# Two buffers of a scan change places, an output copy gets four buffers instead of two, and three small pieces of work move between engines

## The chip, the cores and the metric

The kernel runs on one core of a Trainium2 chip. The core has a matrix engine (PE, with its weight loads shown as PEld), a vector engine (DVE), a scalar engine (ACT), a general engine (POOL), and SyncE (SP), whose queue issues most of the DMA transfers here. Each engine works through its own instructions in order and waits for others by semaphores. The metric is device time in microseconds (us). A part of the time lies around the profiled span, from the first to the last instruction.

## What is computed

Two independent parts, whose results stand side by side in the output (1 x 2048 x 896, bf16). S = 2048 positions, D = 448 features.

Part A is a state-space convolution with complex diagonal state:

```
Lam_bar = exp(dt * Lam);  B_bar = ((Lam_bar - 1) / Lam) * B
Bu = x @ B_bar^T
for t in range(2048):
    h = Lam_bar * h + Bu[t];  hs.append(h)
y = 2 * real(hs @ C^T) + x * Dskip
```

Part B is attention in which a position sees eight positions at distances 0, 2, ..., 14 behind it, with 16 heads of 28 features:

```
q, k, v = split(x @ wqkv)
logits[s, w] = q[s] . k[s - 2 w] / sqrt(28)     (s - 2 w >= 0)
out = (sum over w of softmax(logits)[s, w] * v[s - 2 w]) @ wo
```

## The kernel before, in words

Both parts share one core and are woven together by hand. Part B's projections for q and k run first (`proj_t`), then v (`proj`), with DVE making the products q x k (`products`, L312) and PE summing them over the features of a head (`sums`, L323). `softmax` works on one half `hf` of the positions at a time: PE turns the logits (tile `lgs`, L355), DVE takes the maximum, ACT the exponential into tile `e` (L364), PE sums, and DVE multiplies `e` with the reciprocal into `attn` (L374). `pv` is DVE's main work: for each quarter of the positions, eight multiplications of `attn` with `vd` (L414) and seven additions (L417). A finished quarter is turned by a DMA transpose into `oT` (`tail`, L430), multiplied with `wo` on PE (`wo_ps`, L437), copied by ACT into a buffer `yb` (two buffers; the last quarter writes into places of `ya` instead) and stored from SP's queue (L441). One quarter makes four such copies and stores (`i` and `odd`).

Part A holds 448 complex states in seven groups `m`, and reads the positions as 512 columns of four consecutive positions `b`. Level 1 (`level1_halves`, `level1`) builds for `b` = 0 to 3 the state inside a group of four from PE matmuls (L130, L638, L642), copied into `h` by ACT. `scan` carries states over the columns: for the groups 0 to 3, then 4 and 5, then 6, it sums four columns on PE (L673, L676), ACT copies them into the first of a pair of tiles `pbuf` (L678), and in seven steps PE adds the tile shifted by 1, 2, 4, ... columns (L683), and ACT copies the result to the other tile of the pair (L686). Tiles with one tag share one place in memory; the next tile of that place may be written when the last reader of the tile before is done. The first scan's pair lives in the places of `e` and `lgs`; the other scans' pairs have their own. POOL clears a strip in front of each `pbuf` (L628). `ends` makes the remaining columns (`gt`, L702) into `G`; `setup_c` makes the output matrix `Ccat` (L613).

`correct(b, m, eng)` then adds to `h[b]` of group `m` what comes from earlier columns: a matmul with `G` (L711). With `eng` "V", DVE adds the result to `h` (L715). With "A", PE adds `h` itself by a second matmul with the identity (L710), and ACT copies the sum back (L713). `y` makes the output of a quarter of the columns: the skip term with the diagonal `Dg` (L727), seven matmuls with `Ccat` (L731), ACT's copy into `ya` (L734), a store (L735). `Dg` is made in `skip`: PE turns the row Dskip (L583), one engine copies it to `dsk` (L585), ACT scales the identity with it (L588).

Order of the work: PE's instructions are chained by hand (`chain`; `lanes` for the projections; the list `line` at the end). In the last stage `line` holds seven corrections by ACT, the second quarter's `wo` matmuls, the `y` sums for `b` = 3, 0, 1, the third quarter's, `y` for 2 and the last quarter's; one correction for DVE is put in after each 1.55 us of estimated PE work. DVE's instructions of the last two quarters are chained too (`vchain`); `each` counts them, and from the fifth on sets a correction behind each. What is not chained is ordered by a planner when the kernel is built, from priorities (the order in the program) and its own estimates of time; it writes each engine's queue, SP's too, so a different program can give a different order.

Of the kernel before, what the change touches and what calls it, by code (L numbers as in the profile page):

```python
# [15 lines left out]
bf16 = mybir.dt.bfloat16  # L16

S = 2048
D = 448
T = 16  # L20
NCH = 128
# [13 lines left out]
NM = 7  # L35
# [3 lines left out]
PAD = 64  # L39
# [121 lines left out]
class PartB:  # L161
# [260 lines left out]
    def tail(self, hf, jl0, acc, last):  # L422
        nc, pool, cx = self.nc, self.pool, self.cx
        if self.oT is None:
            self.oT = pool.tile([KA, 2, 14, NCH], bf16, name="oT", tag="bX")
        oT, flat = self.oT[:, self.oi % 2], acc.rearrange("p j d h -> p (j d h)")
        self.oi += 1
        n = 7 if last else 14
        for c in range(0, 14, n):
            nc.sync.dma_start_transpose(oT[:, c:c + n], flat[:, c * KA:(c + n) * KA])  # L430

        def out(i):
            done = []
            for odd in range(2):
                ps = cx.ps([NCH, D], f32, "wo_ps", "lg")
                for k in range(KT):
                    done.append(nc.tensor.matmul(ps[:], lhsT=oT[:, 7 * i + 3 * odd + k, :], rhs=self.wo_p[:, odd, k, :],  # L437
                                                 start=(k == 0), stop=(k == KT - 1)).ins)
                yb = cx.ya[:, 4 + 2 * i + odd] if last else pool.tile([NCH, D], bf16, name="yb", tag="yb", bufs=2)[:]
                cx.ev("V" if last and odd else "A", yb, ps[:])  # L440
                nc.sync.dma_start(self.out_b[:, hf * HJ + jl0 + 2 * i + odd, :], yb)  # L441
            return done

        return out if last else lambda: [out(i) for i in range(2)]


class PartA:
# [132 lines left out]
    def skip(self):  # L580
        nc, ident = self.nc, self.cx.ident
        ptd = self.cx.ps([KA, KT], bf16, "pt_d", "lg")
        self.cx.chain(nc.tensor.transpose(ptd[:], self.drow[:], ident[0:KT, 0:KT]).ins)  # L583
        dsk = self.pool.tile([KA, KT], f32, name="dsk")
        nc.vector.tensor_copy(dsk[:], ptd[:])  # L585
        self.Dg = self.pool.tile([KA, KT, KA], bf16, name="Dg")
        for k in range(KT):
            nc.scalar.activation(self.Dg[:, k, :], ident[:], ACT.Copy, scale=dsk[:, k:k + 1])  # L588
# [32 lines left out]

    def alloc_scan(self):
        pool = self.pool
        self.pbuf = [[pool.tile([NCH, m1 - m0, PAD + NCH], bf16, name=f"pbuf{m0}{i}", tag=f"pbuf{m0}{i}" if m0 else ("e", "lgs")[i]) for i in range(2)]
                     for m0, m1 in MH]
        for pb in self.pbuf:
            for t_ in pb:
                self.cx.order(self.nc.gpsimd.memset(t_[:, :, 0:PAD], 0.0).ins, self.cx.relay, "NoSync")  # L628
        self.G = pool.tile([NCH, NM, 2 + NF], bf16, name="G", tag="q0")
        self.cx.order(self.nc.gpsimd.memset(self.G[:, :, 0:1], 0.0).ins, self.cx.relay, "NoSync")  # L630
# [109 lines left out]
def body(ctx: ExitStack, tc: tile.TileContext, A_x, A_Lre, A_Lim, A_Bre, A_Bim, A_Cre, A_Cim, A_logdt, A_Dskip,  # L740
         B_x, B_wqkv, B_wo, out):
    nc = tc.nc
    pool = ctx.enter_context(tc.tile_pool(name="sb", bufs=1))
    psum = ctx.enter_context(tc.tile_pool(name="ps", bufs=1, space=bass.MemoryType.PSUM))
    out_v = out[0].rearrange("(p j) e -> p j e", j=T)
    cx = Ctx(tc, pool, psum)
    b = PartB(cx, B_x, B_wqkv, B_wo, out_v[:, :, D:2 * D])
    a = PartA(cx, A_x, A_Lre, A_Lim, A_Bre, A_Bim, A_Cre, A_Cim, A_logdt, A_Dskip, out[0].rearrange("(n b) e -> n b e", b=4)[:, :, 0:D])
# [98 lines left out]
        a.ends(mh)  # L847
    cx.ya = pool.tile([NCH, 8, D], bf16, name="ya", tag="cn")
    line, extra, steps = [], [], []
    todo = [(b_, m) for b_ in (1, 2) for m in range(NM)]  # L850

    def each(ins):
        cx.vchain(ins)
        steps.append(ins)
        if len(steps) >= 5 and todo:
            extra.extend(a.correct(*todo.pop(0), "V"))

    def wo_line(lists):
        return [(i, 0.19) for l_ in lists for i in l_]

    for m in range(NM):
        line += a.correct(0, m, "A")
    line += wo_line(wo[1]())
    deque(b.pv(0, at0, 0, 4, each=each), 0)
    deque(b.pv(0, at0, 4, 8, True, each=each), 0)
    for b_, r in itertools.product((3, 0, 1, 2), range(4)):
        line += a.y(r, b_)
# [41 lines left out]
```

## Time and profile before

| | |
|---|---|
| median of 3 runs | 150.92 us (150.15 to 151.6) |
| the profiled execution | 150.87 us |
| its span | 148.9 us |
| PE busy | 137.5 us, 1258 matmuls |
| DVE busy | 124.5 us, 156 instructions |
| ACT busy | 90.1 us, 197 instructions |
| POOL busy | 10.5 us |
| mean granted PE clock | 0.989 |

A line of the order of time gives start, duration, engine, line of the kernel, operation, output and inputs with their size, and in brackets the idle time of the engine before it with what ended it. Consecutive instructions of one form are merged ("x6"). A line of the table of waits gives the engine and line that waited, the one it waited for, the total in us, how often, and the longest. A line for a stretch A:B gives its length, then busy time and count for PE, PEld, DVE, ACT and POOL, then the granted PE clock (1.00 is full), the DMA engines' share and GB/s.

### The profile page before, as it was taken

What the parts mean: (1) busy time and instruction counts of PE and PEld (TensorE: products, weight loads), DVE (VectorE), ACT (ScalarE), POOL (GpSimd) and SP (SyncE); (2) the same over time, 40 slices, a digit from 0 to 9 for tenths busy, and PEclk for the clock granted to TensorE, in tenths of its full rate; (3) what the DMA queues carried; (4) which work ended last, traced back from release to release, by engine and by line L of the source; (5) the groups of instructions that cost most, each with busy time, mean ns of one, the idle gap of its engine ahead of it and who ended that gap; (6) DMA issues with size and microseconds to landing.
All of it is one profiled execution on the core that took longest, in us unless ns stands there. A gap on an engine that the chain in (4) does not pass through costs nothing.

```text
span 148.9 us, 3301 instructions
## 1 busy us (share of the span) xinstructions
PE 137.5 (92%) x1258; PEld 78.3 (53%) x1258; DVE 124.5 (84%) x156; ACT 90.1 (61%) x197; POOL 10.5 (7%) x108
## 2 busy tenths in 40 slices
PE   6999999999999989999789999929999999999971
PEld 2565435445666555466455556518656555555430
DVE  4689639989999889999999999940799999999411
ACT  3668685878585685635599978646963233354320
POOL 7211000000000001000020000000000000000000
PEclk9999999999999999999999999996999999999999
DMA  4999899899948699900033000341013128123473
GB/s 111 316 206 132 207 188 143 160 129 207 189 97 168 109 241 253 218 1 0 0 64 64 0 0 0 74 122 57 0 43 112 63 57 194 62 92 122 67 203 106
DMA packets 45166, 17.03 MB, mean 114 GB/s; under 512 B 37267, under 2 KB 44769, under 8 KB 45151
## 3 DMA queue, kind: packets, MB, share of 16 engines
q1 hardware_dynamic: 44586, 16.36, 53.3%
q10 hardware_dynamic: 565, 0.46, 1.2%
q8 instruction: 10, 0.16, 0.5%
q14 instruction: 5, 0.04, 0.1%
HBM read 3.91 MB, written 3.67 MB: 51 GB/s over the span
## 4 chain that ended last, share of the span: by engine, by line
PE 67%; DVE 18%; ACT 6%; DMA 4%; issue 2%; POOL 0%; ACTq 0%; DVEq 0%; POOLq 0%
PE qk_ps L130 16%; PE y_ps L731 14%; PE wo_ps L437 5%; DVE pvb L414 5%; PE l L638 5%; PE v_ps L130 5%; PE lg L323 4%; DVE pvb L417 4%; PE gt L702 3%; PE co L711 3%; PE warm L73 2%; DVE pr L312 2%; ACT pbuf L686 2%; PE y_ps L727 2%; DMA out_dram<-yb 2%; DMA oT<-pvb 2%
## 5 line engine op out<-in xcount | busy, mean ns | idle before, releaser
L414 DVE TENSOR_TENSOR pvb<-attn,vd 128x1792 bf16<-128x1792 bf16 (+1 forms) x33 | 34.3, 1062 | 0.0
L417 DVE TENSOR_TENSOR pvb<-pvb 128x1792 bf16<-128x1792 bf16 (+1 forms) x29 | 30.7, 1060 | 0.3
L130 PE MATMUL qk_ps<-xbT,wqkv_nat 64*128 64x512 bf16 (+1 forms) x210 | 24.0, 335 | 0.7 <-POOL spot L139 0.3
L312 DVE TENSOR_TENSOR pr<-q,kd 128x3072 bf16<-128x3072 bf16 x11 | 19.1, 1756 | 3.5 <-ACT q L156 3.1
L731 PE MATMUL y_ps<-Ccat,h 128*128 128x448 bf16 x84 | 18.5, 353 | 0.0
L734 ACT CAST ya<-y_ps 128x448 bf16<-128x448 f32 x16 | 8.5, 532 | 16.4 <-PE y_ps L731 15.8
L130 PEld LDWEIGHTS <-wqkv_nat 64*128 64x128 bf16 x210 | 11.1, 94 | 10.5 <-POOL spot L139 3.1
L130 PE MATMUL l1h<-xaT,Bcat 64*128 64x512 bf16 x112 | 15.4, 377 | 0.0
L715 DVE TENSOR_TENSOR h<-co,h 128x512 bf16<-128x512 f32 x14 | 9.7, 690 | 6.5 <-PE co L711 6.5
L437 PE MATMUL wo_ps<-wo_p,oT 128*128 128x448 bf16 x64 | 14.0, 352 | 1.1 <-ACT ya L734 0.6
L638 PE MATMUL l<-xaT,Bcat 128*128 128x512 bf16 x48 | 13.6, 379 | 0.0
L130 PE MATMUL v_ps<-wqkv_nat,xbT 64*128 64x448 bf16 x112 | 13.1, 361 | 0.0
L156 ACT CAST kd<-qk_ps 128x512 bf16<-128x512 f32 (+4 forms) x26 | 10.4, 423 | 4.5 <-PE qk_ps L130 4.3
L156 ACT CAST q<-qk_ps 128x512 bf16<-128x512 f32 (+2 forms) x23 | 9.9, 455 | 1.7 <-PE qk_ps L130 1.4
L156 ACT CAST yb<-wo_ps 128x448 bf16<-128x448 f32 x12 | 6.5, 542 | 6.6 <-DMA out_dram<-yb 4.5
L683 PE MATMUL l<-pbuf,mat 128*128 128x127 bf16 (+6 forms) x49 | 6.4, 223 | 4.4 <-ACT pbuf L686 3.0
L686 ACT CAST pbuf<-l 128x512 bf16<-128x512 f32 (+2 forms) x21 | 8.8, 420 | 2.5 <-PE l L683 2.4
L731 PEld LDWEIGHTS <-h 128*128 128x128 bf16 x84 | 7.4, 98 | 5.4
L156 ACT CAST vd<-v_ps 128x448 bf16<-128x448 f32 x16 | 7.6, 528 | 3.7 <-PE v_ps L130 3.5
L312 DVE TENSOR_TENSOR kd<-q,kd 128x3072 bf16<-128x3072 bf16 x5 | 8.8, 1756 | 1.2 <-ACT q L156 1.2
L130 PEld LDWEIGHTS <-Bcat 64*128 64x128 bf16 x112 | 7.0, 94 | 5.3 <-issue 0.4
L139 POOL MEMSET spot<- 1x1 f32 x63 | 5.6, 88 | 58.9 <-PE qk_ps L130 25.4
(133 smaller groups left out, 216.6 us busy)
## 6 DMA issues: line engine op xcount, KB each, us to landing
out_dram<-ya SPq DMA_DIRECT2D x20, 112.0 KB, 1.7
out_dram<-yb SPq DMA_DIRECT2D x12, 112.0 KB, 1.7
vd<-vd SPq DMA_DIRECT2D x1, 784.0 KB, 5.8
wqkv_nat<-in_B_wqkv_dram SPq DMA_DIRECT2D x2, 336.0 KB
vd<-vd SPq DMA_DIRECT2D x1, 588.0 KB
xn<-in_B_x_dram SPq DMA_DIRECT2D x2, 224.0 KB, 3.4
cn<-in_A_C_re_dram SPq DMA_DIRECT2D x4, 98.0 KB, 3.0
cn<-in_A_C_im_dram SPq DMA_DIRECT2D x4, 98.0 KB, 3.4
```

Of the source, the lines that this page charges most:

```text
L130: ins = mm(g["ps"], lhsT=l_, rhs=r_, start=first, stop=not (g["left"][0] or g["left"][1]), skip_group_check=True).ins
L156: return self.nc.scalar.copy(out, in_).ins
L312: self.queued(V.tensor_tensor(pr, q[0][:, qu].unsqueeze(2).to_broadcast([KA, KT - 1, 4, n]), self.shifted(self.kT[:, 2 * i + qu], s), op=A ...
L414: each(V.tensor_tensor(t_[:, c0:c1], at[:, w, jl0 + c0:jl0 + c1, :].unsqueeze(2).to_broadcast([NCH, c1 - c0, DH, H]), self.vd[:, off + c0: ...
L417: ins = V.tensor_tensor(acc[:, c0:c1], acc[:, c0:c1], t_[:, c0:c1], op=ALU.add).ins
L437: done.append(nc.tensor.matmul(ps[:], lhsT=oT[:, 7 * i + 3 * odd + k, :], rhs=self.wo_p[:, odd, k, :], start=(k == 0), stop=(k == KT - 1)) ...
L638: nc.tensor.matmul(ps[:], lhsT=self.Bcat[:, m, k, :], rhs=self.xT[:, b, k, :], start=(k == 0), stop=(b == 0 and k == KT - 1))
L683: nc.tensor.matmul(ps[:, m - m0, shf:], lhsT=M[T << s_][:, m, :], rhs=src[:, m - m0, PAD:PAD + NCH - shf], start=False, stop=True, skip_gr ...
L686: nc.scalar.copy(dst[:, :, PAD:], ps[:])
L715: cx.vchain(nc.vector.tensor_tensor(h, ps[:], h, op=ALU.add).ins)
L731: out.append(nc.tensor.matmul(ps[:], lhsT=self.state(m, r, b), rhs=self.C[:, m, :], start=False, stop=(m == NM - 1), skip_group_check=True ...
L734: nc.scalar.copy(ya, ps[:])
```

## The change

Five edits. The output copies of part B get four buffers `yb` instead of two. The copy of the skip row goes from DVE to ACT. The first scan's pair changes places: its first tile now lies where `lgs` was and its second where `e` was. The two corrections (1, 0) and (1, 1) leave DVE's list, 14 long before and 12 now, and are made by ACT behind its seven. DVE's first correction comes behind the seventh counted step of part B instead of the fifth.

```diff
-                yb = cx.ya[:, 4 + 2 * i + odd] if last else pool.tile([NCH, D], bf16, name="yb", tag="yb", bufs=2)[:]
+                yb = cx.ya[:, 4 + 2 * i + odd] if last else pool.tile([NCH, D], bf16, name="yb", tag="yb", bufs=4)[:]
...
-        nc.vector.tensor_copy(dsk[:], ptd[:])
+        nc.scalar.copy(dsk[:], ptd[:])
...
-        self.pbuf = [[pool.tile([NCH, m1 - m0, PAD + NCH], bf16, name=f"pbuf{m0}{i}", tag=f"pbuf{m0}{i}" if m0 else ("e", "lgs")[i]) for i in range(2)]
+        self.pbuf = [[pool.tile([NCH, m1 - m0, PAD + NCH], bf16, name=f"pbuf{m0}{i}", tag=f"pbuf{m0}{i}" if m0 else ("lgs", "e")[i]) for i in range(2)]
...
-    todo = [(b_, m) for b_ in (1, 2) for m in range(NM)]
+    todo = [(b_, m) for b_ in (1, 2) for m in range(NM)][2:]
...
-        if len(steps) >= 5 and todo:
+        if len(steps) >= 7 and todo:
...
-    for m in range(NM):
-        line += a.correct(0, m, "A")
+    for b_, m in [(0, m) for m in range(NM)] + [(1, 0), (1, 1)]:
+        line += a.correct(b_, m, "A")
```

## The prediction

> **What bounds the kernel now.** I read the page's first and fourth parts, then the table of waits, then the instructions in order of time around the largest waits.
>
> ```profile
> span 148.9 us, 3301 instructions
> ...
> PE 137.5 (92%) x1258; PEld 78.3 (53%) x1258; DVE 124.5 (84%) x156; ACT 90.1 (61%) x197; POOL 10.5 (7%) x108
> ...
> PE 67%; DVE 18%; ACT 6%; DMA 4%; issue 2%; POOL 0%; ACTq 0%; DVEq 0%; POOLq 0%
> ```
>
> PE is busy 137.5 of 148.9 us and makes two thirds of the chain that ended last. So the time is the PE's work plus the places at which PE stands still or runs slowly, unless DVE (124.5 us) comes to end later than PE. The table of waits (total, times, longest) names those places:
>
> ```profile
> DVE h L715 <- PE co L711: 6.5, 1, 6.5
> ...
> ACT yb L156 <- DMA out_dram<-yb: 4.5, 4, 2.9
> ...
> ACT pbuf L678 <- DVE attn L374: 1.8, 1, 1.8
> ```
>
> Behind both of ACT's waits stands one of PE. In order of time, the later pair, which is the larger:
>
> ```profile
> 94.29 1.53 SPq L430 DMA_TRANSPOSE oT<-pvb  x1
> ...
> 95.87 15.17 SPq L441 DMA_DIRECT2D out_dram<-yb  x6
> ...
> 97.43 1.09 DVE L417 TENSOR_TENSOR pvb<-pvb 128x1792 bf16<-128x1792 bf16 x1
> 98.99 0.53 ACT L156 CAST yb<-wo_ps 128x448 bf16<-128x448 f32 x1 [2.90 <-DMA out_dram<-yb]
> ...
> 99.74 0.21 PE L683 MATMUL l<-pbuf,mat 128*128 128x112 bf16 x1 [2.87 <-ACT pbuf L686]
> ```
>
> The third `yb` copy finds both buffers taken. The first buffer's store stood in SP's queue behind the transpose, began at 95.87 and released ACT at 98.99. The in-order ACT held the last scan's `pbuf` copies behind that copy, and PE waited 2.87 us for them. DVE finished its fifth step of part B at 97.43 + 1.09 = 98.52 and then waited 6.50 us for the first correction.
>
> **The change part by part.** Everything is taken off or put on 150.87 us, the profiled execution's own time (span 148.9, so 1.97 lie around it); the median of the three runs shown is 150.92.
>
> *Four `yb` buffers.* The four copies of a pass (two `i`, two `odd`) no longer reuse a buffer, so the wait on a store goes from this pass; the next pass comes over 10 us later (behind the correction casts, which end at 109.01 by a row below), when those stores have landed. Both copies that waited remain, at 0.53 us each on ACT, in front of scan copies. PE gains at most its 2.87 us, and at least 2.87 - 2 x 0.53 = 1.81 if the two casts now delay the scan in full. I take **-2.87**: in the stretch below ACT (the fourth pair of columns) was busy 1.49 of 4 us, so the casts find room there.
>
> ```profile
> 94.00:98.00 4.00, 2.72 (x19) 1.59 (x17) 3.93 (x5) 1.49 (x5) 0.00 (x0) 1.00 0.70 144
> ```
>
> *The clock behind that wait.* One form of `gt` matmul, before and after the clock recovers:
>
> ```profile
> 100.68 0.52 PE L702 MATMUL gt<-h,ident 128*128 128x384 bf16 x1
> ...
> 104.03 0.33 PE L702 MATMUL gt<-h,ident 128*128 128x384 bf16 x1
> ```
>
> It takes 0.52 us at first and 0.33 later. The stretches below give the granted clock in the column behind POOL: 0.61 right behind the wait, 0.98 after.
>
> ```profile
> 92.77:109.01 16.24, 13.21 (x89) 8.94 (x88) 9.67 (x12) 11.40 (x30) 0.00 (x0) 0.89 0.24 58
> ...
> 98.98:103.05 4.07, 3.31 (x23) 2.62 (x23) 0.00 (x0) 3.08 (x10) 0.00 (x0) 0.61 0.19 59
> 103.05:108.39 5.34, 5.34 (x36) 3.59 (x35) 3.36 (x5) 4.98 (x11) 0.00 (x0) 0.98 0.00 1
> ```
>
> PE was busy 3.31 us there, and would have needed 3.31 x 0.61 / 0.98 = 2.06 at the later clock: 1.25 us. ACT, though, was busy 3.08 of those 4.07 us with the copies that these matmuls feed, so some of it will not show. Between 0 and -1.25 I take **-0.7**.
>
> The Trainium skill, "TensorE: Matmul & The Clock Gate", in "What's actually happening", lets the clock fall only after an idle window of about 3.4 us. By that rule an idle of 2.87 us would cost no clock, this term would be 0 and the sum 146.1. The rows above differ from it: the clock was 0.61 behind a wait of 2.87 us.
>
> *The scan's homes.* `pbuf` 0 of the first scan lay in the home of `e`, which the multiplication into `attn` reads last; it moves to the home of `lgs`, whose last readers are the `lt` matmuls near 55 us (quoted with the skip row below).
>
> ```profile
> 71.99 0.53 ACT L156 CAST Ccat<-c_ps 128x448 bf16<-128x448 f32 x1
> ...
> 73.53 0.69 DVE L374 TENSOR_TENSOR attn<-e,rec 128x1024 bf16<-128x1024 bf16 x1
> ...
> 74.31 0.58 ACT L678 CAST pbuf<-l 128x512 bf16<-128x512 f32 x1 [1.78 <-DVE attn L374]
> ...
> 74.94 0.28 PE L683 MATMUL l<-pbuf,mat 128*128 128x127 bf16 x2 [1.38 <-ACT pbuf L678]
> ...
> 75.63 0.62 ACT L686 CAST pbuf<-l 128x512 bf16<-128x512 f32 x1
> ```
>
> The first copy (74.31) can start 1.78 us earlier; now the second copy (75.63) is the one that needs `e`, and it can start at 74.31, 1.32 us earlier. The clearing of the padding on POOL takes the same two homes in the same order, and no scan step reads it. PE loses its wait of 1.38 but may wait some tenths at the second step. Behind it both are full (3.92 and 3.94 of 4 us):
>
> ```profile
> 78.00:82.00 4.00, 3.92 (x29) 2.29 (x28) 4.00 (x6) 3.94 (x9) 0.00 (x0) 1.00 0.37 69
> ```
>
> So what they gain at the start is carried along, unless DVE, which doesn't get earlier, delivers the late steps' `mat` tiles just in time. Bounds 0 and -1.78; I take **-1.2**.
>
> *Two more corrections on ACT.* Each takes two matmuls instead of one:
>
> ```profile
> 104.55 0.38 PE L711 MATMUL co<-G,mat 128*128 128x512 bf16 x1
> ...
> 104.98 0.38 PE L711 MATMUL co<-G,mat 128*128 128x512 bf16 x1
> 105.03 0.69 DVE L715 TENSOR_TENSOR h<-co,h 128x512 bf16<-128x512 f32 x1 [6.50 <-PE co L711]
> 105.40 3.61 ACT L713 CAST h<-co 128x512 bf16<-128x512 f32 x7
> ```
>
> From 104.55 to 104.98 PE makes two of them, so a correction with one matmul more costs 0.215 us more, two of them **+0.43** on PE. On ACT two casts of 3.61 / 7 = 0.52, 1.03 in all. In 92.77 to 109.01 ACT was busy 11.40 of 16.24 us; with 12.43 in a stretch shortened by the terms above to about 13.1 it is nearly full. Behind these casts wait `yb` copies of the next pass and the buffers of the first `y` sums; that is a rival below.
>
> *Corrections later.* DVE does two steps of about 1.06 us inside the 6.50 us in which it stood. It reaches its first correction at 98.52 + 2.1 = 100.6, and PE's first `co` would come at 104.55 - 2.87 - 0.7 - 1.2 = 99.8, so DVE waits no more. Its later work shrinks by those two steps and by two corrections of 0.6 (start to start of its pieces below):
>
> ```profile
> 109.90 0.69 DVE L715 TENSOR_TENSOR h<-co,h 128x512 bf16<-128x512 f32 x1
> 110.50 1.09 DVE L417 TENSOR_TENSOR pvb<-pvb 128x1792 bf16<-128x1792 bf16 x1
> ```
>
> It ends at 139.61 - 4.4 - 2.1 - 1.2 = 131.9 instead of 139.61. That is no term by itself, since PE ends later; it pays at the end:
>
> ```profile
> 138.99 0.62 DVE L417 TENSOR_TENSOR pvb<-pvb 128x896 bf16<-128x896 bf16 x1
> ...
> 141.12 1.23 SPq L430 DMA_TRANSPOSE oT<-pvb  x1
> ...
> 141.83 1.25 PEld L437 LDWEIGHTS <-oT 128*128 128x128 bf16 x8 [1.04 <-DMA oT<-pvb]
> 141.83 1.69 PE L437 MATMUL wo_ps<-wo_p,oT 128*128 128x448 bf16 x8 [0.60 <-ACT ya L734]
> ...
> 144.03 1.69 PE L437 MATMUL wo_ps<-wo_p,oT 128*128 128x448 bf16 x8 [0.52 <-DMA oT<-pvb]
> ```
>
> PE's last two groups wait 0.60 and 0.52 us, each for a transpose (the second one landed 2.9 us after its issue). The first wait is put down to a `ya` copy that ended at the same moment; the weight load beside it names the transpose. With DVE done 7 us earlier and PE 4 to 5, the transposes land first: **-1.12** (bounds 0, if SP's queue keeps them behind late stores, and -1.12).
>
> *The skip row's copy on ACT.*
>
> ```profile
> 54.37 0.15 DVE L585 CAST dsk<-pt_d 128x4 f32<-128x4 bf16 x1
> ...
> 54.57 0.41 PE L355 MATMUL lt<-ident,lgs 128*128 128x128 bf16 x4 [0.46 <-DVE dsk L585]
> ...
> 54.62 1.28 ACT L588 ACTIVATE Dg<-ident,dsk 128x128 bf16<-128x128 bf16 x4 [0.23 <-DVE dsk L585]
> ```
>
> ACT sat idle 0.23 us before `Dg`, waiting for this very copy, so it can make it within a few tenths of the same moment. If it runs earlier, PE gains up to its 0.46; if a `vd` copy of 0.5 stands in front, PE loses as much. I take 0, with -0.46 and +0.5 as ends.
>
> Sum: -2.87 - 0.7 - 1.2 + 0.43 - 1.12 = -5.46, so 150.87 - 5.46 = **145.4 us**. All best ends give -2.87 - 1.25 - 1.78 + 0.43 - 1.12 - 0.46 = -7.05, or 143.8; all worst ends -1.81 + 0.43 + 0.5 = -0.88, or 150.0.
>
> **The rivals.**
>
> *Only the buffer wait goes.* ACT, nearly full, becomes what paces PE between 92 and 105 us, and the start won at the scan is lost again before it. Then the clock and homes terms are 0 and half of the tail's stays: -2.87 + 0.43 - 0.56 = -3.0, so 147.9. For it speaks ACT at 12.43 of 13.1 us; against it that PE's four `co` buffers let it run ahead of ACT by some 2 us.
>
> *It doesn't do what it says.* The third copy is free of its buffer but the order that the planner writes leaves other waits of the same size, say behind PE's `wo_ps` sums: about 150.4. Against it: ACT's release at 98.99 stands 3.1 us after the store's issue, and the last of those sums was made well before:
>
> ```profile
> 95.63 0.54 PE L437 MATMUL wo_ps<-wo_p,oT 128*128 128x448 bf16 x2
> ```
>
> *Slower: the first scan starves PE.* The planner writes the order of each engine anew. With the first copy free from 72.5 us it can set the scan's steps ahead of the level-1 matmuls which now fill the pauses between steps:
>
> ```profile
> 76.43 0.41 PE L683 MATMUL l<-pbuf,mat 128*128 128x126 bf16 x4
> ...
> 77.79 0.41 PE L683 MATMUL l<-pbuf,mat 128*128 128x124 bf16 x4
> ```
>
> A step comes 1.36 us after the one before and uses 0.41 of PE; 0.95 is filled. Empty in all seven steps, that is 6.65 us on PE, and the homes term goes: 145.4 + 1.2 + 6.65 = 153.3. It decides in favour of slower from (153.3 - 150.87 = 2.4 less) 4.2 us of such gaps, or 0.6 a step. Against it: code and priorities of the two kinds of work are unchanged, and the PE now interleaves them evenly.
>
> **How the numbers follow.** A forecast within 143.8 to 147.2 gets 0.64, only the buffer wait (147.2 to 149.4) 0.20, no effect 0.07, slower 0.08; 0.01 is below. The range takes the first two: 143.8 to 149.2. About 1%, 149.4 and 152.4, is what a measurement can tell from no change. Faster 0.85, same 0.07, slower 0.08.
>
> **What would show it.** Right: no `yb` copy waits for a store near 95 us; no PE wait over 1 us between 92 and 105, and a granted clock near 1 there; the first `pbuf` copy starts near 72.6 and the second near 74.3; first `co` near 99.8; DVE's wait ahead of its first correction under 1 us; DVE's last step near 132; no wait of the last two `wo_ps` groups for a transpose. Wrong: PE gaps between the first scan's steps, ACT without idle time from 92 on with PE waiting for it, or the last transposes issued behind late `ya` stores.

## The result, and the profile after

The changed kernel took 145.52 us in the median of four runs (145.12 to 145.92), against 150.53 for the kernel before: a ratio of 0.966, with a 95% interval of 0.960 to 0.972. The forecast was 145.4 in a range of 143.8 to 149.2. The profiled execution took 145.12 us. In the table of the experiments the medians are of all executions, while the ratios leave out four that ran slow: two of the changed kernel with two buffers, one of the kernel before with its homes exchanged (473.77 us) and one of the kernel before.

The page after, and its waits (total, times, longest):

```profile
span 143.2 us, 3302 instructions
...
PE 137.2 (96%) x1260; PEld 78.0 (54%) x1260; DVE 123.2 (86%) x153; ACT 90.9 (63%) x200; POOL 10.5 (7%) x108
```

```profile
ACT yb L156 <- PE wo_ps L437: 2.3, 8, 0.4
...
PEld L683 <- DVE mat L607: 0.7, 1, 0.7
```

PE does the same work, and two matmuls more, in 5.7 us less span: its share rose from 92 to 96%. No `yb` copy waits for a store any more, no wait on `attn` stands in front of the first scan copy, and the only new wait of a scan step is one on a `mat` tile. In order of time, the first scan, the `yb` copies, the first corrections and the end:

```profile
73.39 0.59 ACT L678 CAST pbuf<-l 128x512 bf16<-128x512 f32 x1 [0.26 <-PE l L676]
...
74.20 0.69 DVE L374 TENSOR_TENSOR attn<-e,rec 128x1024 bf16<-128x1024 bf16 x1
...
74.98 0.59 ACT L686 CAST pbuf<-l 128x512 bf16<-128x512 f32 x1
...
94.48 0.53 ACT L156 CAST yb<-wo_ps 128x448 bf16<-128x448 f32 x1
...
96.54 3.36 SPq L441 DMA_DIRECT2D out_dram<-yb  x4
...
99.74 0.39 PE L711 MATMUL co<-G,mat 128*128 128x512 bf16 x1
...
100.24 1.09 DVE L417 TENSOR_TENSOR pvb<-pvb 128x1792 bf16<-128x1792 bf16 x1
...
101.24 0.68 DVE L715 TENSOR_TENSOR h<-co,h 128x512 bf16<-128x512 f32 x1
...
131.43 2.57 SPq L430 DMA_TRANSPOSE oT<-pvb  x2
131.94 0.62 DVE L417 TENSOR_TENSOR pvb<-pvb 128x896 bf16<-128x896 bf16 x1
...
135.34 1.49 PE L731 MATMUL y_ps<-Ccat,h 128*128 128x448 bf16 x7
...
136.67 3.31 PE L437 MATMUL wo_ps<-wo_p,oT 128*128 128x448 bf16 x16
```

The third `yb` copy starts at 94.48, two microseconds before any store of this pass is issued (96.54). DVE reaches its first correction without idle time. Both last transposes are issued together, and PE runs the last sixteen `wo_ps` matmuls as one piece, with no wait.

This execution reached `attn` at 74.20, the one before at 73.53; the first 70 us differ by such tenths from one execution to the next. So distances from `attn` are compared below. To the first correction: before 104.55 - 73.53 = 31.02 us, after 99.74 - 74.20 = 25.54, a gain of 5.48. Two stretches from the first `yb` copy to the first correction, the first of before, the second of after (length; busy time of PE, PEld, DVE, ACT, POOL; PE's clock):

```profile
92.77:104.55 11.78, 8.74 (x68) 6.45 (x66) 5.68 (x6) 7.05 (x22) 0.00 (x0) 0.86 0.34 80
```

```profile
92.36:99.74 7.38, 7.16 (x67) 5.49 (x66) 7.31 (x8) 6.77 (x22) 0.00 (x0) 1.00 0.48 110
```

Of the 11.78 - 7.38 = 4.40 us, PE's idle time gives 3.04 - 0.22 = 2.82, and its busy time, for the same matmuls (68 and 67 records of them), 8.74 - 7.16 = 1.58: the clock was 0.86 in one stretch and 1.00 in the other.

### The profile page after: what moved, and what is told of

Its sections match the earlier page's. It is cut to its first block, busy times and chain, and to the rows that moved or that the text cites. A ratio compares the mean times of both kernels' runs of the same rounds, so it can differ in the third digit from the quotient of the medians.

```text
span 143.2 us, 3302 instructions
## 1 busy us (share of the span) xinstructions
PE 137.2 (96%) x1260; PEld 78.0 (54%) x1260; DVE 123.2 (86%) x153; ACT 90.9 (63%) x200; POOL 10.5 (7%) x108
## 4 chain that ended last, share of the span: by engine, by line
PE 69%; DVE 23%; ACT 3%; issue 2%; POOL 0%; DVEq 0%; ACTq 0%; POOLq 0%
PE qk_ps L130 16%; PE y_ps L731 15%; DVE pvb L414 8%; PE wo_ps L437 7%; DVE pvb L417 6%; PE v_ps L130 5%; PE lg L323 5%; PE l L638 5%; PE co L711 3%; PE warm L73 3%; DVE pr L312 2%; DVE mat L607 2%; PE y_ps L727 2%; PE gt L702 2%; PE l L683 2%
## 5 line engine op out<-in xcount | busy, mean ns | idle before, releaser
L731 PE MATMUL y_ps<-Ccat,h 128*128 128x448 bf16 x84 | 17.9, 353 | 0.0
L130 PEld LDWEIGHTS <-xbT 64*128 64x128 bf16 x112 | 7.3, 145 | 4.1 <-issue 1.3
L437 PEld LDWEIGHTS <-oT 128*128 128x128 bf16 x64 | 6.0, 98 | 5.5 <-issue 0.6
L649 ACT CAST h<-l1h 128x512 bf16<-128x512 f32 x12 | 6.3, 602 | 3.5 <-PE l1h L130 3.5
```

The costliest lines, as they stand in the source:

```text
L130: ins = mm(g["ps"], lhsT=l_, rhs=r_, start=first, stop=not (g["left"][0] or g["left"][1]), skip_group_check=True).ins
L649: self.nc.scalar.copy(h, ps)
L731: out.append(nc.tensor.matmul(ps[:], lhsT=self.state(m, r, b), rhs=self.C[:, m, :], start=False, stop=(m == NM - 1), skip_group_check=True ...
```

## The experiments

Twelve kernels ran, in three groups, each group beside the kernel before on its own chip. "Two" and "four" are the `yb` buffers; "homes" are the exchanged homes; "corrections" are nine by ACT, twelve by DVE, from the seventh step. The kernel before has one median in each group. That of the last is lower because fewer of its executions there had the drop of the clock (see "The clock by itself"), so between groups the times compare better than the ratios.

| kernel | median us | before, same chip | ratio, 95% interval |
|---|---|---|---|
| the changed kernel again | 145.38 | 151.27 | 0.963 (0.959 to 0.966) |
| changed, homes as before | 146.39 | 151.27 | 0.970 (0.966 to 0.974) |
| changed, seven and fourteen corrections | 145.78 | 151.27 | 0.965 (0.961 to 0.969) |
| changed, all corrections as before | 146.52 | 151.27 | 0.970 (0.966 to 0.974) |
| changed, two buffers | 151.55 | 151.36 | 1.002 (0.998 to 1.005) |
| before, homes exchanged | 151.31 | 151.36 | 1.003 (0.999 to 1.007) |
| before, four buffers | 147.31 | 151.36 | 0.974 (0.970 to 0.978) |
| before, PE kept busy in the wait | 149.72 | 151.36 | 0.990 (0.987 to 0.993) |
| before, first stores from ACT's queue | 146.95 | 150.38 | 0.974 (0.969 to 0.979) |
| before, corrections of the change | 151.25 | 150.38 | 1.005 (1.001 to 1.008) |
| changed, skip row's copy on DVE | 144.93 | 150.38 | 0.961 (0.957 to 0.964) |
| changed, eight and thirteen corrections | 144.85 | 150.38 | 0.960 (0.957 to 0.964) |

### The buffers: alone, and taken away

Alone on the kernel before:

```diff
-... name="yb", tag="yb", bufs=2)[:]
+... name="yb", tag="yb", bufs=4)[:]
```

> The kernel before with four yb buffers and nothing else. Theory: the buffer wait of 2.9 us and most of the slow clock behind it (1.25) go, 4.1 to 4.4 us on PE up to the first correction; but DVE is then the later one at the end, as it still waits for its first correction and has all fourteen: it ends about 4 us earlier than before, so the last transposes stay as late against PE as they were and the tail's waits of 1.1 us stay. 146.2 to 146.5. Rival (the clock drop is covered by ACT's copies): 147.4 to 147.7.

Measured: 4.0 us faster (147.31 against 151.36). The time lies between the theory's 146.2 to 146.5 and the rival's 147.4 to 147.7. From the order of time and a stretch of this kernel:

```profile
74.14 0.68 DVE L374 TENSOR_TENSOR attn<-e,rec 128x1024 bf16<-128x1024 bf16 x1
...
100.76 0.39 PE L711 MATMUL co<-G,mat 128*128 128x512 bf16 x1
...
138.31 1.69 PE L437 MATMUL wo_ps<-wo_p,oT 128*128 128x448 bf16 x8 [0.86 <-DMA oT<-pvb]
...
140.70 1.69 PE L437 MATMUL wo_ps<-wo_p,oT 128*128 128x448 bf16 x8 [0.71 <-DMA oT<-pvb]
```

```profile
93.38:100.76 7.38, 7.16 (x68) 5.49 (x66) 5.68 (x6) 6.76 (x22) 0.00 (x0) 1.00 0.53 126
```

The first correction comes 100.76 - 74.14 = 26.62 us behind `attn`: 4.40 earlier than before, at the upper end of what was expected, with the clock at 1.00. The waits at the end not only stay, they are 1.57 us instead of 1.12, which takes 0.45 of it back. That, and a kernel before that took 151.36 here instead of the 150.87 from which the theory counted, is what its time missed; the rival's reason, a clock drop covered by ACT's copies, is not borne out.

The changed kernel with two buffers, the same line the other way round:

> The changed kernel with two yb buffers again. Theory (the third yb copy is tied through the first store to the transpose in front of it in SP's queue, and that to DVE, which the change does not make earlier): the wait of ACT comes back and is longer than 2.9 us by the 1.1 us that PE and ACT now arrive earlier, the granted clock falls again, the first correction comes near 104.5 whatever the scan gained; of the change only the tail's 1.4 us less 0.43 for ACT's corrections remains: 149.5 us. Rival (the terms add up independently): the scan's 1.1 us stays too, 148.4.

Measured: 151.55, no faster than before, and 2 us above the theory. In order of time:

```profile
98.95 0.53 ACT L156 CAST yb<-wo_ps 128x448 bf16<-128x448 f32 x1 [3.60 <-DMA out_dram<-yb]
...
135.25 2.57 SPq L430 DMA_TRANSPOSE oT<-pvb  x2
...
137.91 1.02 SPq L441 DMA_DIRECT2D out_dram<-yb  x2
...
141.98 0.53 ACT L156 CAST yb<-wo_ps 128x448 bf16<-128x448 f32 x1 [4.36 <-DMA out_dram<-yb]
```

The first wait is back as expected, longer (3.60 us instead of 2.90). What was not expected is a second one: with DVE done earlier, the planner puts both last transposes ahead of three of the third quarter's four stores in SP's queue, and with two buffers ACT stands 4.36 us on such a store, with three `ya` copies behind it. So four buffers are worth 4.0 us alone and about 6 us (151.55 - 145.38) in the changed kernel.

The corrections alone on the kernel before show the same thing from the other side:

```diff
-    todo = [(b_, m) for b_ in (1, 2) for m in range(NM)]
+    todo = [(b_, m) for b_ in (1, 2) for m in range(NM)][2:]
...
-        if len(steps) >= 5 and todo:
+        if len(steps) >= 7 and todo:
...
-    for m in range(NM):
-        line += a.correct(0, m, "A")
+    for b_, m in [(0, m) for m in range(NM)] + [(1, 0), (1, 1)]:
+        line += a.correct(b_, m, "A")
```

> The kernel before with the corrections of the change alone (nine by ACT, twelve by DVE from its seventh step), two buffers, old homes. Theory (DVE's earlier end lets the planner set the last transposes ahead of yb stores in SP's queue; with two buffers ACT then stands on a store again, near the end): ACT waits 3 to 5 us for a store behind the last transposes and the time is that of before or longer, 150.5 to 152. Rival (the tail's waits of 1.1 us go at the price of 0.43): 149.9 to 150.6, no wait on a store over 1.5 us near the end.

Measured: 151.25 us, 1.005 of before. That is no loss: the clock drop was in nine of these ten executions, but in only seven of the 17 of the kernel before on this chip, and those seven have a median of 151.28. The wait near the end is there:

```profile
135.53 2.57 SPq L430 DMA_TRANSPOSE oT<-pvb  x2
...
138.19 1.02 SPq L441 DMA_DIRECT2D out_dram<-yb  x2
...
141.70 0.53 ACT L156 CAST yb<-wo_ps 128x448 bf16<-128x448 f32 x1 [3.82 <-DMA out_dram<-yb]
```

### Is it the number of buffers or the place in the queue?

The kernel before with two buffers; only the first pass's four stores change their queue:

```diff
-                nc.sync.dma_start(self.out_b[:, hf * HJ + jl0 + 2 * i + odd, :], yb)
+                (nc.scalar if (hf, jl0) == (1, 0) else nc.sync).dma_start(self.out_b[:, hf * HJ + jl0 + 2 * i + odd, :], yb)
```

> The kernel before with two yb buffers, but the first pass's four stores are issued from ACT's queue instead of SP's, so that they don't stand behind the transpose. Theory (the wait came from the place of the store in SP's queue, not from two buffers being too few): each store starts right behind its copy, lands within 3 us, ACT waits at most 1 us for a buffer, the clock stays up, first correction near 101 to 102, time 147 to 148.5, like four buffers alone (147.3) or up to 1 us behind, for four issues of about 0.4 us on ACT. Rival (a store takes too long for two buffers wherever it is issued): the wait stays at 2 to 3 us, 149.5 to 151.5.

Measured: 146.95 us, where four buffers gave 147.31 on another chip. The first store is issued behind its copy, ahead of the transpose:

```profile
93.65 0.53 ACT L156 CAST yb<-wo_ps 128x448 bf16<-128x448 f32 x1
94.26 0.36 ACTq L441 DMA_DIRECT2D out_dram<-yb  x1
95.16 1.53 SPq L430 DMA_TRANSPOSE oT<-pvb  x1
...
96.92 0.65 ACT L156 CAST yb<-wo_ps 128x448 bf16<-128x448 f32 x1
```

In the kernel before, the same copy and DVE's last addition of that quarter stood so:

```profile
92.77 0.53 ACT L156 CAST yb<-wo_ps 128x448 bf16<-128x448 f32 x1
...
93.16 1.10 DVE L417 TENSOR_TENSOR pvb<-pvb 128x1792 bf16<-128x1792 bf16 x1
```

The copy was done at 93.30, the addition at 94.26; the transpose went out at 94.29 and the store behind it at 95.87, 2.57 us behind the copy. In this pass two buffers were enough for stores that leave at once. The cause of the wait was a store that had to pass a transpose which itself waited for DVE; four buffers cover that, and another queue removes it. The order of PE's work changed in this kernel too (one correction came ahead of the last `gt` groups), so its first correction is not compared with the others'.

### The clock by itself

The kernel before, with PE kept busy in the wait by thirteen matmuls on zeros, whose sums nobody reads; the wait itself stays.

```diff
...
+        for i in range(13):
+            ins = nc.tensor.matmul(wp[:], lhsT=cx.wz[:, 0:NCH], rhs=cx.wz[:], start=True, stop=True).ins
+            cx.order(ins, prev, "NoSync")
+            prev = ins
...
```

> The kernel before, with thirteen more matmuls on zeros (2.8 us, their sums are not used) in PE's queue where it waits for the yb buffer. The wait of ACT stays. Theory (the slow clock behind the wait costs about 1 us by itself): the granted clock stays near 1 behind the wait, the gt groups take 0.5 us each instead of 1.0, the first correction comes 0.7 to 1.3 us earlier and the time is 0.7 to 1.3 us shorter, 149.3 to 149.9. Rival (ACT's copies pace that stretch, the clock is covered): within 0.3 us of before.

Measured: ratio 0.990, 1.5 us faster than before. In order of time, and a stretch:

```profile
73.89 0.68 DVE L374 TENSOR_TENSOR attn<-e,rec 128x1024 bf16<-128x1024 bf16 x1
...
97.07 2.97 PE L889 MATMUL warm<-wz 128*128 128x512 bf16 x12
99.33 0.53 ACT L156 CAST yb<-wo_ps 128x448 bf16<-128x448 f32 x1 [2.87 <-DMA out_dram<-yb]
...
100.13 0.32 PE L702 MATMUL gt<-h,ident 128*128 128x384 bf16 x1
...
104.01 0.38 PE L711 MATMUL co<-G,mat 128*128 128x512 bf16 x1
...
140.88 1.69 PE L437 MATMUL wo_ps<-wo_p,oT 128*128 128x448 bf16 x8 [0.20 <-DMA oT<-pvb]
...
142.82 1.69 PE L437 MATMUL wo_ps<-wo_p,oT 128*128 128x448 bf16 x8 [0.25 <-DMA oT<-pvb]
```

```profile
98.98:103.05 4.07, 3.59 (x32) 2.81 (x32) 0.00 (x0) 3.43 (x11) 0.00 (x0) 1.00 0.19 61
```

ACT still waited 2.87 us for the store, but the clock behind it is 1.00 instead of 0.61, and the `gt` matmul takes 0.32 us instead of 0.52. The first correction comes 30.12 us behind `attn`, 0.90 earlier than before: that much is shown to be the clock's. The other 0.67 us lie at the end, where the last two groups waited 0.20 and 0.25 us instead of 0.60 and 0.52. There the first of the last two transposes held SP's queue for a shorter time, first here, then before:

```profile
137.95 1.23 SPq L430 DMA_TRANSPOSE oT<-pvb  x1
```

```profile
138.48 1.91 SPq L430 DMA_TRANSPOSE oT<-pvb  x1
```

DVE's last step starts 34.44 us behind the first correction in both, so DVE is not the reason; what is, stays open. So of the 1.5 us, work that computes nothing brought 0.90.

The kernel before gives a second test. In 16 of its 51 executions in the three groups (2 of 11, 4 of 23 and 10 of 17) the mean granted clock was 0.996 or more, in the other 35 it was 0.985 to 0.989. The medians are 150.1 and 151.4 us. So the drop behind this wait comes often but not every time, and with it the whole takes about 1.3 us more. That PE stood as long in the executions without it is not shown, since none of them was traced. In the two kernels whose traces show PE standing for 3.6 us at this place (the changed one with two buffers and the one with the homes alone), the mean clock was 0.989 or less in all 19 executions of usual length.

### The homes: alone, and taken away

```diff
-... if m0 else ("e", "lgs")[i]) ...
+... if m0 else ("lgs", "e")[i]) ...
```

> The kernel before with the first scan's homes exchanged and nothing else; the order of every engine's queue is that of before. Theory (as above, the stall ends with a store that hangs on DVE): the second scan copy is 1.3 us earlier, ACT's wait for the store grows from 2.9 to about 4.0 us, and the time stays within 0.3 us of before. Rival (the gain is carried to the end as in a sum): 1.1 us faster, 149.4.

> The changed kernel with the first scan's two homes as before. Theory (what the first scan gains is carried through to the end, because PE and ACT are full behind it): the first scan's second copy is 1.3 us later, the first correction 1.1 us later, the time 145.5 + 1.1 = 146.6. Rival (ACT or a late mat tile paces the stage up to 100 us, so the gain is lost on the way): 145.5, within 0.3.

Alone on the kernel before (the order of every queue is unchanged there): 151.31 against 151.36, nothing. Taken away from the changed kernel: 146.39 against 145.38, so it is worth 1.0 us there, and the first correction is 1.11 us later (26.65 instead of 25.54 us behind `attn`). In the kernel before the gain runs into the store:

```profile
73.42 0.58 ACT L678 CAST pbuf<-l 128x512 bf16<-128x512 f32 x1 [0.26 <-PE l L676]
74.15 0.68 DVE L374 TENSOR_TENSOR attn<-e,rec 128x1024 bf16<-128x1024 bf16 x1
...
99.23 0.53 ACT L156 CAST yb<-wo_ps 128x448 bf16<-128x448 f32 x1 [3.60 <-DMA out_dram<-yb]
```

The scan starts earlier, and ACT's wait grows from 2.90 to 3.60. The store hangs on the transpose, the transpose on DVE, and DVE was not made earlier: the store is issued 22.34 us behind `attn` with the homes exchanged and without.

### The corrections in the changed kernel

First with seven by ACT and fourteen by DVE, then with DVE's start at the fifth step as well (the lines above the other way round); then with eight and thirteen (`[1:]` and only `(1, 0)`).

> The changed kernel with seven corrections by ACT and fourteen by DVE as before, DVE's first still behind the seventh step. Theory (PE is the bound from the first correction on, and a correction by ACT costs it one matmul more): 2 x 0.215 less PE work, 145.1 us; DVE ends at 132.6 + 1.2 = 133.8 and its transposes still land before PE's last groups ask for them. Rival (DVE's later end takes the gain back at the last transposes): 145.5 to 146.5, with a wait of the last wo_ps groups on a transpose.

> The changed kernel with all corrections as before: seven by ACT, fourteen by DVE from its fifth step on. Theory: DVE reaches its first correction near 99 and waits for it about 1.2 us, so it ends 1.0 to 1.2 us later than with the start behind the seventh step, near 135; the last transpose lands near 138.5 where PE would ask for it near 138, so 0 to 0.8 us is lost: 145.1 to 145.9. Rival (the place where DVE's corrections begin carries a large part of the gain): 147 or more.

> The changed kernel with eight corrections by ACT and thirteen by DVE, between the changed kernel (nine, twelve: 145.4, no wait at the end) and seven and fourteen (145.8, a wait of 0.7 us on a transpose). Theory (PE and DVE with its transposes end at the same time, so one gains what the other loses): PE's list 0.2 shorter, DVE's end 0.6 later, a wait of 0 to 0.4 us in front of the last groups, 145.2 to 145.5. Rival (the order of SP's queue decides, not the length of DVE's work): if a yb store comes between the last two transposes, 145.7 to 146.

Measured: 145.78, 146.52 and, on another chip, 144.85. Seven and fourteen, the first correction and the end:

```profile
100.07 0.38 PE L711 MATMUL co<-G,mat 128*128 128x512 bf16 x1
...
132.82 1.23 SPq L430 DMA_TRANSPOSE oT<-pvb  x1
...
134.14 0.53 SPq L441 DMA_DIRECT2D out_dram<-yb  x1
134.77 1.75 SPq L430 DMA_TRANSPOSE oT<-pvb  x1
...
135.26 1.49 PE L731 MATMUL y_ps<-Ccat,h 128*128 128x448 bf16 x7
...
137.46 3.32 PE L437 MATMUL wo_ps<-wo_p,oT 128*128 128x448 bf16 x16 [0.71 <-DMA oT<-pvb]
```

The rival is right here: PE's list is shorter by the expected amount (the last `y` group starts 35.19 us behind the first correction instead of 35.60), but DVE ends later, a `yb` store comes between the last two transposes, and PE waits 0.71 us. Against 145.38 the time alone does not tell the two kernels apart. With all corrections as before the waits are 0.64 and 0.59 us, and the time is 1.1 us longer than the changed kernel's: 0.6 us more than the theory gave and 0.5 less than its rival, so DVE's start at the fifth step costs 0.7 us beside seven and fourteen from the seventh. With eight and thirteen only a weight load of the last groups waits, 0.3 us, and their matmuls start 1.33 us behind the last `y` group as in the changed kernel, which did not run on this chip. Beside the changed kernel with the skip row on DVE, which did (144.93), 144.85 is no faster version that these runs can show.

### The skip row

```diff
-        nc.scalar.copy(dsk[:], ptd[:])
+        nc.vector.tensor_copy(dsk[:], ptd[:])
```

> The changed kernel with the skip row's copy on DVE again. Theory (ACT and DVE make it at the same moment): PE's wait in front of the second lt group is 0.4 to 0.5 us either way, time within 0.3 us of the changed kernel's 145.4. Rival (DVE, which now has no idle time behind it, carries every tenth to the end): 0.1 to 0.3 longer, not to be told from the first by the time alone, but by the start of the first step of part B behind attn.

Measured: 144.93, ratio 0.961, the same as its neighbour of that chip (144.85). PE's wait is 0.46 us with DVE and 0.38 with ACT; the first is from this kernel, the second from the changed one. The sign that was named agrees: part B's first step behind `attn` starts 1.19 us after it here and 1.20 in the changed kernel.

```profile
54.90 0.41 PE L355 MATMUL lt<-ident,lgs 128*128 128x128 bf16 x4 [0.46 <-DVE dsk L585]
```

```profile
55.17 0.41 PE L355 MATMUL lt<-ident,lgs 128*128 128x128 bf16 x4 [0.38 <-ACT dsk L585]
```

## Why the prediction was right, step by step

**The buffers, -2.87: right in cause and close in size.** PE's idle time in the stretch fell by 2.82 us. That the two `yb` copies find room on ACT held: they cost the scan nothing that the stretch shows.

**The clock, -0.7: right in cause, too small.** The busy time of the same matmuls fell by 1.58 us, more than the end of -1.25 that was given. That end scaled PE's 3.31 busy us with 0.61, the mean over a stretch that begins with 0.76 us in which PE still stood at a clock of 1.00. While PE worked, the clock was 0.52 (the kernel before):

```profile
99.74:103.05 3.31, 3.31 (x23) 2.62 (x23) 0.00 (x0) 2.33 (x8) 0.00 (x0) 0.52 0.23 73
```

With that, 3.31 - 3.31 x 0.52 / 0.98 = 1.55. The reason given for a smaller value, that ACT's copies cover part of it, is true only while ACT is late: with the wait kept and the clock restored, 0.90 of it arrived at the first correction. Once the wait was gone too, all 1.58 did. The two terms were not independent. The forecast started from an execution that had the drop; against one without it the gain is about 1.3 us less.

The Trainium skill, "TensorE: Matmul & The Clock Gate", in "What's actually happening", wants an idle window of about 3.4 us before the clock falls; by it this term would have been 0. The runs decide against it here: the wait of 2.87 us with an idle PE was followed by a clock of 0.61, the same wait with a busy PE by 1.00, and 35 of 51 executions of the kernel before have the lower mean clock.

**The homes, -1.2: right, with the condition that was named.** The second scan copy came 74.98 - 74.20 = 0.78 us behind the start of `attn` instead of 75.63 - 73.53 = 2.10: 1.32 earlier, as worked out. At the sixth step PE met a `mat` tile of DVE that was just being made, and about 0.2 of the gain stayed there; 26.62 - 25.54 = 1.08 us reached the first correction. What the prediction did not say is that this term depends on the first: alone it was worth nothing.

**Two more corrections on ACT, +0.43: right.** Taking them back shortens PE's list by 0.41 us.

**DVE and the tail, -1.12: right in cause, a little small.** DVE ended at 132.56 instead of the forecast 131.9, which is 58.4 us behind `attn` as forecast, with no wait at its first correction, and the waits in front of the last two groups went. In the kernel before the last `y` group started here:

```profile
139.74 1.49 PE L731 MATMUL y_ps<-Ccat,h 128*128 128x448 bf16 x7
```

The second group had stood 144.03 - 139.74 = 4.29 us behind the start of the last `y` group. After, the sixteen matmuls start 136.67 - 135.34 = 1.33 us behind it, and eight of them take about 1.5, so the gain is 1.4 to 1.5. It had a price that the prediction did not see: the order of SP's queue changes with it, and with two buffers the wait on a store that comes of it takes half of the tail's gain or more: the second group stands 3.64 us behind the last `y` group with the corrections alone and 4.19 in the changed kernel with two buffers, and both take the time of before.

**The skip row, 0: right.**

The sum on the profiled execution was 145.41 and came out at 145.12. By the terms as measured it is -4.40 - 1.08 + 0.41 - 1.45 = -6.5, of which the later start of that execution (0.67 at `attn`) took a part back. So the gain behind `attn` was 1.1 us larger than the forecast's, most of it the clock's term, and that the time came within 0.3 us is in part luck.

**The rivals.** "Only the buffer wait goes" fell: from the first `yb` copy to the end of the correction casts PE was busy 12.62 of 12.84 us while ACT was busy 12.08, so ACT was indeed nearly full, but PE hardly waited for it. "It doesn't do what it says" fell too: no `yb` copy waits for a store, and waits of that size are gone. "The first scan starves PE" fell too: the steps are filled as before, and the order of PE there did not change. The 4.2 us of gaps named with it are where the time would equal that of before; slower by the 1% that a measurement can tell would have taken 1.5 us more.

## What to carry to other kernels

A wait on a buffer can be a wait on a queue: look at what stands in front of the store that has to free the buffer, since another queue or more buffers then do the same. Gains in front of such a wait are worth nothing until it is gone, and an edit that ends work earlier can change what the planner queues behind it, so edits that look additive are worth testing in pairs. Add to a PE wait what the matmuls behind it lose at a lower clock.

## What the runs showed of the hardware

The matrix engine's clock was 0.52 of full over the 3.31 us behind an idle time of only 2.87 us, and 2.97 us of matmuls on zeros in that idle time kept it at 1.00. The kernel's first correction came 0.90 us earlier by this alone. The drop was not in every execution: 35 of 51 of the same kernel had it, and they took about 1.3 us more. A DMA transpose held SP's queue for 1.23 to 2.34 us in these runs, and two issued together for 2.57, where a store took 0.33 in the median.
